# Two sets of fifteen tiny loads on the sync queue of a cached-attention and MLP decode kernel

## The chip, the cores and the metric

The kernel runs on one core of a Trainium2 chip. The metric is the device time of one execution in microseconds (us). The kernel before has a median of 211.23 us over two runs (211.19 to 211.27).

## What is computed

One decode step: a layer norm of the input, then a grouped-query attention over a window of a key/value cache, and beside it a small MLP, summed. Cut to what matters:

```python
# x: 4 x 1 x 576; k_cache, v_cache: 4 x 16 x 8192 x 128; wq: 576 x 4096; wo: 4096 x 576
# w1, w2: 576 x 576; w3: 576 x 4608; w4: 4608 x 576; all bfloat16
def _A_ref(x, k_cache, v_cache, wq, wo):
    W = min(4096, max(256, Sk // 4))                  # 2048 positions
    q = (x @ wq).reshape(B, Sq, Hq, Dh).transpose(0, 2, 1, 3)
    k = jnp.repeat(k_cache[:, :, Sk - W:, :], rep, axis=1)
    v = jnp.repeat(v_cache[:, :, Sk - W:, :], rep, axis=1)
    p = _softmax(jnp.einsum("bhqd,bhkd->bhqk", q, k) * (Dh ** -0.5), axis=-1)
    o = jnp.einsum("bhqk,bhkd->bhqd", p, v)
    return o.transpose(0, 2, 1, 3).reshape(B, Sq, Hq * Dh) @ wo

def _B_ref(x, w1, w2, w3, w4):
    ...
    x1 = x + hs
    h2 = _gelu(_layernorm(x1, axis=-1) @ w3) @ w4
    return x1 + h2

xn = _layernorm(A_x)
return A_x + _A_ref(xn, ...) + _B_ref(xn, ...)
```

With a sequence of one position the padded shifts of the MLP's first part are all zeros, so hs is zero, and w1 and w2 don't enter the result. The kernel before never reads them.

## The kernel before

The 16 key/value heads are worked through one at a time. For each head there is a key tile K and a value tile V, each of 128 partitions with 16 KB, 2 MB in all; the 128 partitions hold four batch entries of 32 row groups, and the tiles live in one pool of six buffers (tag kv). The weights come in larger pieces: wq (4.5 MB), four quarters of wo (wo0 to wo3, 1.1 MB each), w3 (5 MB) and w4 (5 MB in six pieces, with 128 of its rows split off into a small tile called x4). wq, w3 and w4 take turns in one buffer.

All of these loads, except for the input's, are issued by one engine, SP, on the sync queue, in an order written out by hand: the schedule is manual, and an engine runs its instructions in the order of the program. `flush_loads` (L568) walks the list `order`: K0, K1, K2, V0, K3, V1, K4, V2, w3, K5, V3, K6, wo1, V4, and so on, with a quarter of wo ahead of every fourth value tile. Around the two places of the change the order is K9, V7, K10, wo2, V8, K11 ... and, at the end, V13, two x4 rows, V14, three small x4 loads, V15, three x4 rows of one partition, and the six pieces of w4 (`load_w4`, L147, issued by L153). `load_kv` (L100) issues a key or value tile by L103; `x4_rows` (L160) issues the small loads by L164 (20 partitions), L167 (4), L170 (12) and L174 (1).

The loop over t = 0 to 15 (L591) works on several heads at once: it transposes and scores K of head t (DVE L256, PE L369), takes the softmax of head t-1, multiplies head t-2 by its V (PE L426), and scales, sums and projects heads t-3 and t-4. At the end of an iteration `flush_loads` is called again for the buffers that came free, those of K(t) and V(t-2). SP then waits, load by load, for the engine that last read the buffer.

There is a second thing that an issue on SP waits for. Each DMA reports its landing on a semaphore, and the framework that builds the program hands out eight of these semaphores in turn over the DMAs, in program order. An issue that takes a semaphore waits until the DMA that had it before, eight places earlier, has landed, unless SP has already waited for that landing or a later one on it. These waits stand in the built program's list of SP instructions.

The kernel ends with the last heads' remaining steps, the matmuls with w4 as its pieces land (`mlp_out`, PE L215), two copies to the output tile (L684, L686) and its store (L687).

The pool `pad` (L75) holds a tile of 384 bytes per partition that nothing reads or writes.

Of the kernel before, what the change touches and what calls it, by code (L numbers as in the profile page):

```python
# [11 lines left out]
BF16 = mybir.dt.bfloat16  # L12
F32 = mybir.dt.float32
# [5 lines left out]
PAD = 96  # L19
# [3 lines left out]
def kernel(  # L23
# [14 lines left out]
    nc = tc.nc  # L38
    P = 128
# [33 lines left out]


    pad = ctx.enter_context(tc.tile_pool(name="pad", bufs=1))  # L75
    pad.tile([P, PAD], F32, name="pad")
    kvp = ctx.enter_context(tc.tile_pool(name="kv", bufs=NKV))
    wp = ctx.enter_context(tc.tile_pool(name="w", bufs=1))
    wop = ctx.enter_context(tc.tile_pool(name="wo", bufs=2))
# [20 lines left out]
    def load_kv(kind, h):  # L100
        win = k_win if kind == "K" else v_win
        t = kvp.tile([P, NC, Dh], BF16, tag="kv", name=f"{kind.lower()}n")
        nc.sync.dma_start(out=t[:].rearrange("p c d -> p (c d)"),  # L103
                          in_=win[:, h].rearrange("b (p c) d -> p b (c d)", c=NC))
        kv_tiles[kind, h] = t
# [17 lines left out]
    def load_wo(p):  # L123
        t = wop.tile([P, WOR, D], BF16, tag="wo", name="wo_sb")
        nc.sync.dma_start(out=t[:].rearrange("p i n -> p (i n)"), in_=wo_src[p])
        wo_tiles[p] = t

    def load_w3():
        t = wp.tile([P, KJ * F + F // 2], BF16, tag="w", name="w3_sb")
        nc.sync.dma_start(out=t[:, 0:KJ * F], in_=B_w3[0:KJ * P, :].rearrange("(p j) f -> p (j f)", j=KJ))  # L130
        nc.sync.dma_start(out=t[:, KJ * F:], in_=B_w3[KJ * P:D, :].rearrange("r (e f) -> (r e) f", e=2))
        w_tiles["w3"] = t
# [14 lines left out]
    def load_w4():  # L147
        t = wp.tile([P, NFM, D], BF16, tag="w", name="w4_sb")
        for lo, hi in zip(W4_PIECES, W4_PIECES[1:]):
            e = lo // NFH  # L150
            n = NFH - e
            src = B_w4[e * (F // 2):e * (F // 2) + P * n, :].rearrange("(p i) n -> p i n", i=n)
            nc.sync.dma_start(out=t[:, lo:hi, :], in_=src[:, lo - e * NFH:hi - e * NFH, :])  # L153
        w_tiles["w4"] = t

    def load_x4():
        t = kvp.tile([P, NC, Dh], BF16, tag="kv", name="x4")
        w_tiles["x4"] = t[:].rearrange("p c d -> p (c d)")

    def x4_rows(part):  # L160
        t = w_tiles["x4"]
        if part == "A":
            src = B_w4[X0 + 28:F, :].rearrange("(q g i) n -> g q (i n)", q=4, g=5)
            nc.sync.dma_start(out=t[0:NX, XA * D:XS * D], in_=src)  # L164
        elif part == "B":
            src = B_w4[X0:X0 + 16, :].rearrange("(q i) n -> q i n", q=4)[:, 3]
            nc.sync.dma_start(out=t[0:4, (XB + 3) * D:XC * D], in_=src)  # L167
        elif part == "C":
            src = B_w4[X0 + 16:X0 + 28, :].rearrange("(q g) n -> g q n", q=4)
            nc.sync.dma_start(out=t[0:12, XC * D:XA * D], in_=src)  # L170
        else:
            q, lo, hi = part
            src = B_w4[X0 + 4 * q + lo:X0 + 4 * q + hi, :].rearrange("(q i) n -> q (i n)", q=1)
            nc.sync.dma_start(out=t[q:q + 1, (XB + lo) * D:(XB + hi) * D], in_=src)  # L174
# [86 lines left out]
    for kb in range(NQD):  # L261
        nc.gpsimd.tensor_copy(out=sel[:, :, :, kb, :],
                              in_=ident_bf[:].rearrange("p (ib i e) -> p ib e i", ib=2, e=2))
# [19 lines left out]
    with nc.allow_low_precision("zeros and ones"):  # L283
# [7 lines left out]
                          in_=sel_j[:].unsqueeze(1).to_broadcast([P, NG, NJ]))  # L291
# [38 lines left out]
    for r in range(2):  # L330
        nc.vector.tensor_copy(out=q_bf[:, r],
                              in_=qT_ps[:, r].rearrange("p u (g x) -> p g u x", g=NQD)[:, :, :, 0:B])
# [235 lines left out]
    def flush_loads():  # L568
        while pos["n"] < len(order) and pos["free"] > 0:
            kind, h = order[pos["n"]]  # L570
            if kind == "V" and h % WOQ == 0:
                load_wo(h // WOQ)
            if kind == "X":
                load_x4()
            else:
                load_kv(kind, h)
            if kind == "X" or kind == "V" and h > min(X_AFTER):
                for part in X_AFTER.get(h, []):
                    x4_rows(part)
            pos["n"] += 1  # L580
            pos["free"] -= 1
            if (kind, h) == W3_AFTER:
                load_w3()
        if pos["n"] == len(order):
            pos["n"] += 1
            load_w4()

    flush_loads()
    G_AT = 7
    k_transpose(0, 0)  # L590
    for t in range(Hkv):  # L591
# [50 lines left out]
        if hv >= 0:  # L642
            pos["free"] += 1
        flush_loads()

    hl = Hkv - 1
# [71 lines left out]
```

## Time and profile before

| | |
|---|---|
| median of the runs | 211.23 us |
| span of the profiled execution | 209.5 us |
| PE busy | 150.2 us (72%) |
| DVE busy | 113.3 us (54%) |
| ACT busy | 34.9 us (17%) |
| bytes moved by DMA | 87.31 MB, mean 417 GB/s |
| mean granted TensorE clock | 0.868 |
| issue to landing, median: K tiles, V tiles | 25.8 us, 23.0 us |
| SP's longest totals of waiting, L103 | for DVE L387 32.2 us, for PE L426 30.3 us |

The profile is of one execution. The page divides its span into 40 slices and shows, for each engine and for the DMA engines together, the busy share in tenths. A chain of waits is followed back from the last instruction. SPq is SP's own queue: an entry there is the time that an issue took on SP, not the transfer. Time to landing is counted from the issue, so it holds the time that a load stood behind others.

### The profile page before, as it was taken

Reading aid. Unit: us, or ns where it says so; the run is one execution under the profiler, and the core shown is the slowest. Engines: PE = TensorE matmul, PEld = TensorE weight load, DVE = VectorE, ACT = ScalarE, POOL = GpSimd, SP = SyncE. Lnnn points to the kernel's source line nnn. Section 1 sums busy time; section 2 is a strip of 40 time slices with the busy share of each in tenths; the row PEclk is TensorE's granted clock in tenths of the full one; section 3 lists DMA queues with packets and bytes.
Section 4 is the critical chain, followed back from the end, with each engine's and each line's share of the span. In section 5 each row is a group of like instructions: output and inputs, shape, how many; then the busy total and the mean of one; then the engine's idle time right before and its main releaser. Section 6 shows DMA issues by size and latency. Waiting matters only on the chain.

```text
span 209.5 us, 2370 instructions
## 1 busy us (share of the span) xinstructions
PE 150.2 (72%) x972; PEld 57.8 (28%) x972; DVE 113.3 (54%) x156; ACT 34.9 (17%) x72; POOL 9.0 (4%) x32
## 2 busy tenths in 40 slices
PE   0457297698690039759998998589696856999783
PEld 0122132233130003213454332224132312343451
DVE  4511877794910083926607889276849390764110
ACT  7602201112010011110222321102111201023100
POOL 4710000000000000000001200000000000000000
PEclk9999589999797556985999999799879985699699
DMA  7999999999999999999999999999999999999992
GB/s 301 400 422 429 425 429 432 422 438 427 456 422 409 446 419 420 444 444 410 441 422 432 444 405 435 438 444 410 438 429 425 428 445 419 432 438 425 427 407 92
DMA packets 6708, 87.31 MB, mean 417 GB/s; under 512 B 761, under 2 KB 1042, under 8 KB 1706
## 3 DMA queue, kind: packets, MB, share of 16 engines
q1 hardware_dynamic: 6690, 87.17, 97.7%
q8 instruction: 7, 0.11, 0.2%
q10 hardware_dynamic: 8, 0.00, 0.0%
q14 instruction: 3, 0.02, 0.0%
HBM read 87.17 MB, written 0.00 MB: 416 GB/s over the span
## 4 chain that ended last, share of the span: by engine, by line
DMA 76%; PE 18%; DVE 3%; ACT 1%; SPq 1%; issue 1%; DVEq 0%; ACTq 0%
DMA vn<-in_A_v_cache_dram 51%; DMA kn<-in_A_k_cache_dram 12%; DMA w_sb<-in_B_w_dram 7%; DMA wq_sb<-in_A_wq_dram 6%; PE S L369 6%; PE O L426 3%; PE g_ps L499 2%; DVE kt L256 2%; PE q_ps L313 2%; PE oT L439 1%; PE acc L215 1%; PE S L391 1%; DVE qz L345 1%; PE gT_ps L521 1%; SPq L153 1%
## 5 line engine op out<-in xcount | busy, mean ns | idle before, releaser
L369 PE MATMUL S<-kt,qz 128*128 128x512 bf16 x256 | 77.6, 432 | 31.6 <-DVE kt L256 31.6
L256 DVE STREAM_TRANSPOSE kt<-kn 128x2048 int32<-128x2048 int32 x32 | 73.5, 2298 | 25.4 <-DMA kn<-in_A_k_cache_dram 24.0
L369 PEld LDWEIGHTS <-qz 128*128 128x128 bf16 x256 | 23.3, 105 | 64.7 <-issue 47.3
L426 PE MATMUL O<-vn,PT 128*32 128x512 bf16 x256 | 24.3, 424 | 9.7 <-DMA vn<-in_A_v_cache_dram 9.6
L398 ACT ACTIVATE E<-S 128x512 bf16<-128x512 f32 x16 | 9.5, 597 | 73.5 <-PE S L391 73.5
L433 ACT ACTIVATE O_sb<-O,rd 128x512 f32<-128x512 f32 x16 | 11.0, 686 | 63.8 <-DVE rd L416 48.3
L403 DVE STREAM_TRANSPOSE PT<-E 128x512 bf16<-128x512 bf16 x16 | 11.4, 710 | 14.4 <-ACT E L398 14.4
L449 DVE TENSOR_REDUCE on<-oT 128x8 bf16<-128x128 f32 x16 | 4.6, 288 | 22.0 <-PE oT L439 21.9
L426 PEld LDWEIGHTS <-PT 128*32 128x32 bf16 x256 | 5.7, 95 | 33.2 <-issue 22.1
L439 PE MATMUL oT<-ident_w,O_sb 128*128 128x128 f32 x64 | 12.7, 335 | 0.0
L375 DVE TENSOR_REDUCE mx<-S 128x1 f32<-128x512 f32 x16 | 10.5, 657 | 0.9 <-PE S L369 0.9
L439 PEld LDWEIGHTS oT<-ident_w,O_sb 128*128 128x128 f32 x64 | 8.3, 167 | 5.1 <-issue 4.7
L391 PE MATMUL S<-nm,j_row 8*128 8x512 bf16 x16 | 6.8, 428 | 1.8 <-DVE nm L387 1.7
L357 PE MATMUL S<-negbig,ohT 4*128 4x512 bf16 x16 | 6.4, 398 | 0.0
L313 PE MATMUL q_ps<-wq_sb,xnT 128*32 128x512 bf16 x40 | 4.1, 591 | 2.2 <-DMA wq_sb<-in_A_wq_dram 2.2
L215 PE MATMUL acc<-w_sb,gT 128*4 128x288 bf16 x70 | 4.9, 286 | 1.1 <-DMA w_sb<-in_B_w_dram 1.1
L499 PE MATMUL g_ps<-w_sb,ln2T 128*32 128x512 bf16 (+2 forms) x55 | 5.5, 439 | 0.0
L541 POOL TENSOR_TENSOR g_u<-g_x 128x180 f32<-128x180 f32 x1 | 0.5, 486 | 102.5 <-ACT g_x L535 102.5
L215 PE MATMUL acc<-wo_sb,op 128*4 128x288 bf16 x64 | 4.6, 286 | 0.4 <-DVE op L471 0.4
L537 DVE COPY g_x<-gT_ps 128x64 f32<-128x64 f32 x2 | 0.5, 225 | 8.1 <-PE gT_ps L521 8.1
L215 PEld LDWEIGHTS <-gT 128*4 128x4 bf16 (+3 forms) x90 | 3.8, 83 | 3.1 <-issue 1.6
L240 PE MATMUL tp<-ident_bf,first 4*128 4x4 bf16 x8 | 0.6, 172 | 5.3 <-DVE first L227 5.3
(94 smaller groups left out, 79.1 us busy)
## 6 DMA issues: line engine op xcount, KB each, us to landing
kn<-in_A_k_cache_dram SPq DMA_DIRECT2D x16, 2048.0 KB, 25.8
vn<-in_A_v_cache_dram SPq DMA_DIRECT2D x16, 2048.0 KB, 23.0
wo_sb<-in_A_wo_dram SPq DMA_DIRECT2D x4, 1152.0 KB, 38.0
w_sb<-in_B_w_dram SPq DMA_DIRECT2D x1, 4608.0 KB
wq_sb<-in_A_wq_dram SPq DMA_DIRECT2D x1, 4096.0 KB
w_sb<-in_B_w_dram SPq DMA_DIRECT2D x1, 2592.0 KB, 10.9
w_sb<-in_B_w_dram SPq DMA_DIRECT2D x2, 576.0 KB, 34.6
w_sb<-in_B_w_dram SPq DMA_DIRECT2D x1, 864.0 KB
```

What stands on the lines that cost most here:

```text
L215: nc.tensor.matmul(out=acc_of(i), lhsT=lhsT, rhs=rhs[:, i * CW:(i + 1) * CW], start=False, stop=False, skip_group_check=True)
L256: nc.vector.transpose(out=kt[:], in_=src)
L313: nc.tensor.matmul(out=q_ps[r][g * QD:(g + 1) * QD, :], lhsT=xnT[:, k, :], rhs=wq_sb[:, col:col + NW], start=(j == 0), stop=False, skip_gr ...
L369: nc.tensor.matmul(out=S_ps[h][:], lhsT=qz[:, z0:z0 + P], rhs=kt[:, ib, c0:c0 + SC, e:2 * QD:2].rearrange("p c k -> p (c k)"), start=False ...
L375: nc.vector.reduce_max(out=mx[:], in_=S_ps[h][:], axis=AX.X)
L391: nc.tensor.matmul(out=S_ps[h][:], lhsT=j_row[:], rhs=st.pop(("nm", h))[:, 0:1].to_broadcast([NJ, NW]), start=False, stop=False, skip_grou ...
L398: nc.scalar.activation(out=E[h][:].rearrange("p c k -> p (c k)"), in_=S_ps.pop(h)[:], func=ACT.Exp, scale=scale, accum_out=st["rs"][:, h % ...
L403: nc.vector.transpose(out=PT[h][:], in_=E.pop(h)[:])
L426: nc.tensor.matmul(out=O_ps[h][g * QD:(g + 1) * QD], lhsT=PT[h][:, c, :], rhs=vn[:, :, c, :], start=(s == 0), stop=False, skip_group_check ...
L433: nc.scalar.activation(out=O_sb[h][:], in_=O_ps.pop(h)[:], func=ACT.Copy, scale=st.pop(("rd", h)))
L439: nc.tensor.transpose(out=oT[:, s, :], in_=o[:, s, :], identity=ident_w[:, s * NJ:s * NJ + P])
L499: nc.tensor.matmul(out=out, lhsT=ln2T[:, k, :], rhs=rhs, start=(j == 0), stop=False, skip_group_check=True)
```

## The change

After the value tiles of heads 7 and 15 a new function, `load_marks`, issues fifteen loads on the sync queue. The k-th of them (k from 15 down to 1) takes k rows of w1, of 2 + k elements each, into k partitions of a tile that takes the place of the unused pad: 15 x 17, 14 x 16, and so on to 1 x 3 elements of two bytes. Nothing reads that tile. Each load has columns of its own in it; the second set writes the same places again.

```diff
     pad = ctx.enter_context(tc.tile_pool(name="pad", bufs=1))
-    pad.tile([P, PAD], F32, name="pad")
+    mark = pad.tile([P, 2 * PAD], BF16, name="mark")
...
+    def load_marks():
+        at = 0
+        for k in range(15, 0, -1):
+            n = 2 + k
+            nc.sync.dma_start(out=mark[0:k, at:at + n], in_=B_w1[0:k, 0:n])
+            at += n
+
...
                 load_x4()
             else:
                 load_kv(kind, h)
+            if (kind, h) == ("V", 15):
+                load_marks()
             if kind == "X" or kind == "V" and h > min(X_AFTER):
                 for part in X_AFTER.get(h, []):
                     x4_rows(part)
+            if (kind, h) == ("V", 7):
+                load_marks()
             pos["n"] += 1
```

So the first set stands on SP between V7 and K10, and the second between V15 and the last three x4 rows, with w4 behind those. The instructions of the other engines are the same as before.

## The prediction

> **What bounds the kernel now.** I read the page first: the slices, the queue shares, and the chain that ended last.
>
> ```profile
> DMA  7999999999999999999999999999999999999992
> ...
> q1 hardware_dynamic: 6690, 87.17, 97.7%
> ...
> DMA 76%; PE 18%; DVE 3%; ACT 1%; SPq 1%; issue 1%; DVEq 0%; ACTq 0%
> ```
>
> The sync queue's transfers keep the 16 DMA engines busy in every slice but the first and the last. In the middle they move 405 to 456 GB/s, some 430. A 2 MB key or value tile (2.097 MB) therefore takes 2.097/430 = 4.9 us of the stream. PE is busy for 72% of the span, and it is often the engine that waits. So the kernel is one stream of loads with a tail, and the tail is this, from the chain in order of time:
>
> ```profile
> 166.64 22.96 DMA vn<-in_A_v_cache_dram
> ...
> 191.30 14.51 DMA w_sb<-in_B_w_dram
> 205.81 0.04 issue
> 205.85 1.06 PE acc L215 x12
> 206.91 0.43 DVE fin L684
> ```
>
> V14 was issued at 166.64 and landed at 189.60. The last w4 pieces land at about 206, and only some 3.5 us of work follow. A hole in the stream anywhere before that moves the end by its full length, unless something fills it.
>
> What keeps the stream full is SP's lead. This is SP's timeline around the two places of the change (start, length, issue):
>
> ```profile
> 98.67 0.53 SPq L103 DMA_DIRECT2D vn<-in_A_v_cache_dram  x1
> 102.69 0.54 SPq L103 DMA_DIRECT2D kn<-in_A_k_cache_dram  x1
> 105.08 0.33 SPq L125 DMA_DIRECT2D wo_sb<-in_A_wo_dram  x1
> 112.72 0.54 SPq L103 DMA_DIRECT2D vn<-in_A_v_cache_dram  x1
> 117.38 0.54 SPq L103 DMA_DIRECT2D kn<-in_A_k_cache_dram  x1
> ...
> 179.77 0.57 SPq L103 DMA_DIRECT2D vn<-in_A_v_cache_dram  x1
> 184.77 0.82 SPq L174 DMA_DIRECT2D x<-in_B_w_dram  x3
> ```
>
> 98.67 is V7 and 102.69 is K10, which the tile's own rows show landing after
>
> ```profile
> DMA to landing us min/median/max: 22.9/22.9/22.9
> ```
>
> that is, at 125.6. V7 stands one tile ahead of it and lands 4.9 earlier, at 120.7. When V7 lands, K10, wo2, V8 and K11 are already queued: SP leads by 18 us. V15, issued at 179.77, lands after 14.8 us by the same view, at 194.5, and the first w4 piece was queued at 189.62.
>
> **The wait that the change brings.** It is in SP's list of waits (total, times, longest):
>
> ```profile
> SPq L153 <- DMA vn<-in_A_v_cache_dram: 6.8, 2, 4.0
> ...
> SPq L170 <- DMA vn<-in_A_v_cache_dram: 4.6, 1, 4.6
> SPq L174 <- DMA vn<-in_A_v_cache_dram: 4.4, 1, 4.4
> SPq L167 <- DMA wo_sb<-in_A_wo_dram: 2.3, 1, 2.3
> ```
>
> These small loads read and write nothing that a value tile or wo touches. They wait because the eight completion semaphores are handed out in turn and an issue waits until the load eight places earlier has landed. With big loads that rule is harmless, since eight of them are some 35 us of stream. With fifteen tiny ones in a row it is not: in the changed program's list, the eighth tiny load of each set (8 partitions) waits for the value tile just ahead of the set, V7 or V15. SP issues in order, so nothing else can be queued behind that tile until it has wholly landed, and by then every earlier load has landed too. The stream runs dry twice.
>
> **First set, at V7.** The first seven tiny loads (15 to 9 partitions) wait for older loads, the last of them K9, one tile ahead of V7 (about 115.8); they go out before 120.7, under the stream: nothing on the path. Then comes the hole, from V7's landing to K10's data: eight issues (8, 7, 6, 5, 4, 3, 2 and 1 partitions), K10's issue, and the way from issue to data. The issue costs have these nearest rows:
>
> ```profile
> L174 SPq DMA_DIRECT2D x<-in_B_w_dram x5: 240/249/427, 164.0 to 185.3; - x5
> L164 SPq DMA_DIRECT2D x<-in_B_w_dram x1: 907/907/907, 163.0 to 163.0; - x1
> L167 SPq DMA_DIRECT2D x<-in_B_w_dram x1: 248/248/248, 170.0 to 170.0; - x1
> L170 SPq DMA_DIRECT2D x<-in_B_w_dram x1: 837/837/837, 174.9 to 174.9; - x1
> ```
>
> One partition (L174) and four (L167) cost 0.25; twelve (L170) 0.84, twenty (L164) 0.91. Three one-partition issues in 0.82 give 0.29 from start to start, so 0.04 between issues. The bounds for eight are 8 x 0.29 = 2.3 us and 8 x 0.95 = 7.6 us. I take 0.29 for 8, 4, 2 and 1 partitions and 0.88 for 7, 6, 5 and 3, because the cheap rows are counts that are powers of two and the dear ones are not: 4 x 0.29 + 4 x 0.88 = 4.7. It may instead be the dear rows' rearranged sources that cost, and then 2.3 is right.
>
> The restart: the first load of the kernel, 512 KB into an empty queue, landed after 3.3 us, of which 0.524/430 = 1.2 is transfer, so 2.1 us go to the way in and the report of landing. Below, the start's fine windows show the first bytes in 1.50 to 1.75, 0.8 after that issue at 0.74. I take 2.1, since the hole holds both ends: V7's report and K10's way in. K10 waits for the eighth tiny load's slot as well; that lands 2.1 after its issue, under the seven issues that follow (1.8 to 6.7).
>
> The hole is 4.7 + 2.1 = 6.8 us (3.1 to 9.7). Compute doesn't pay again: by 128 the work on K9 and V7 is done, so SP can queue K10, wo2, V8, K11, V9 and K12 at once, 27 us of stream, and the lead is back. Nor does it give back: the stream was full before and is full after.
>
> **Second set, at V15.** The first three wait for V13 and the small x rows, the fourth (12 partitions) for V14, 4.9 us ahead of V15; three more issues follow under V15's own transfer. The eighth waits for V15. After it: the same eight issues, then the three x rows of L174 that now stand behind them (0.82), then w4 and its way in. The hole is 4.7 + 0.8 + 2.1 = 7.6 us (3.9 to 10.5). In the kernel of before SP was stopped here too, but by V14 (L153's 6.8), with V15 still moving. PE's work on V15 falls into this hole and doesn't matter; w4's landing stays last, with the same tail.
>
> **The rest.** The bytes (2 x 1480 elements of two bytes, 6 KB) and their 240 short rows stand in the rings behind V7 and V15 and run in the holes: nothing. The tile mark has the bytes of the tile that it replaces, nobody reads it, and the other engines' instructions are unchanged: nothing.
>
> **The sum.** 6.8 + 7.6 = 14.4 us on the profiled execution's span of 209.5 gives 223.9. The median, 211.23, stands 1.7 above that span, so the time is 225.6 us.
>
> Two rules of the Trainium skill bear on this, both from the page "DMA: Bandwidth & Descriptors". Its section "Issuing engines are not separate DMA queues" says that the time to initiate a DMA on a sequencer is usually small beside the DMA itself; taken as nothing, it would leave 2.1 + 2.1 + 0.8 and 216. The rows speak against it here, since eight issues follow each other with the queue empty. Its section "Anatomy of one DMA" puts a fixed 2.0 us on each DMA; paid one after the other by 30 loads, that would be an estimate of 60 us and 271. Three issues in 0.82 us speak against that.
>
> **The rivals.**
> (a) All tiny issues are cheap, at 0.29: 2.3 + 2.1 and 2.3 + 0.8 + 2.1, 9.6 us, 220.9; with the short restart of 0.8 it is 7.0 and 218.2. For it: four partitions cost no more than one, and the marks' sources are plain rows. Chance 0.28.
> (b) All are dear, at 0.95: 9.7 + 10.5 = 20.2, 231.4. For it: the rows' odd byte counts (34 down to 6), which no row of before has. Chance 0.12.
> (c) One hole only: the tail hides the second, because PE and not w4 is last. PE's waits for w4 pieces are short (1.1 us in all), which speaks for it; but w4's 70 matmuls at a mean of 0.286 us are busy for 4.9 us in all, far less than the 12 us that its pieces (5.16 MB) take to land. 211.2 + 6.8 = 218.0. Chance 0.05.
> (d) Not slower: the slot wait doesn't reach V7's and V15's landings, because the semaphore is satisfied earlier. Then fifteen issues, at most 15 x 0.95 = 14 us, lie under the 22 us from V7's issue to its landing, and SP still leads; set two delays w4's issue by some of 14 us against V15's 14.8. Price 0 to 0.8, time 211 to 212. It decides as soon as K10 goes out before 120.7. Against it: L170 did wait for a value tile. Chance 0.04.
>
> The main case has 0.5, and 0.01 is left for anything else. The range of 219.5 to 230.5 holds the main case with its restart from 0.8 up, most of (a) and part of (b); (c) and (d) fall below. A change of 2% is 4.2 us, about what a measurement of this kernel tells from none: faster 0.01 (nothing above leads there), the same 0.04 (d), slower 0.95.
>
> **What would show it.** In the changed kernel's profile, two DMA slices fall well below 9, near 120 to 127 and 201 to 209; SP's waits gain L160 on vn, about 5 us and more each, with K10 issued after 125 instead of 102.69; the mark's rows give the issue times by size, which settle (a) and (b). Wrong would be K10 issued before V7 lands, DMA slices of 9 throughout, or PE late after the holes, with the stream waiting for buffers.

## The result, and the profile after

The changed kernel takes 224.91 us (median of two runs, 225.55 and 224.26) against 211.23 before: a ratio of 1.0648, 95% interval 1.0575 to 1.0721. The profiled execution has a span of 223.8 us, 14.3 more than before's 209.5. The page's slices, the sync queue's share and the chain by engine:

```profile
DMA  7999999999999999999992799999999999972992
...
q1 hardware_dynamic: 7170, 87.18, 92.3%
...
DMA 71%; DVE 13%; PE 12%; SPq 1%; ACT 1%; issue 1%; DVEq 0%; ACTq 0%
```

The bytes are the same (87.18 MB against 87.17), but the queue's share falls from 97.7% to 92.3%, and slices below 9 stand in two places: near 120 us and near 202 us. The stream ran dry twice. SP's timeline (start, length, issue; a merged row holds the waits between its issues too) shows who let it:

```profile
97.43 0.54 SPq L103 DMA_DIRECT2D vn<-in_A_v_cache_dram  x1
98.01 25.15 SPq L160 DMA_DIRECT2D mark<-in_B_w_dram  x15
123.27 0.54 SPq L103 DMA_DIRECT2D kn<-in_A_k_cache_dram  x1
123.90 0.54 SPq L125 DMA_DIRECT2D wo_sb<-in_A_wo_dram  x1
...
186.78 0.56 SPq L103 DMA_DIRECT2D vn<-in_A_v_cache_dram  x1
191.59 12.33 SPq L160 DMA_DIRECT2D mark<-in_B_w_dram  x15
203.97 1.44 SPq L181 DMA_DIRECT2D x<-in_B_w_dram  x3
205.46 3.16 SPq L153 DMA_DIRECT2D w_sb<-in_B_w_dram  x6
```

K10 goes out at 123.27 instead of 102.69, because SP is among the tiny loads for 25 us. Its waits say on what:

```profile
SPq L160 <- DMA vn<-in_A_v_cache_dram: 22.3, 6, 4.6
...
SPq L160 <- DMA kn<-in_A_k_cache_dram: 9.1, 2, 4.5
...
SPq L181 <- DMA mark<-in_B_w_dram: 0.7, 1, 0.7
```

A tiny load reads w1 and writes a tile of its own, and yet the tiny loads wait 31 us for key and value tiles. The last of those waits in each set ends with V7's or V15's landing. The hole itself, by the microsecond (length, busy time of PE, PEld, DVE, ACT and POOL, granted clock, DMA share, GB/s):

```profile
117.00:118.00 1.00, 1.00 (x5) 0.30 (x4) 0.19 (x2) 0.69 (x2) 0.00 (x0) 1.00 0.99 426
118.00:119.00 1.00, 1.00 (x9) 0.54 (x9) 1.00 (x2) 0.00 (x0) 0.00 (x0) 1.00 0.61 231
119.00:120.00 1.00, 1.00 (x12) 0.22 (x9) 1.00 (x1) 0.00 (x0) 0.00 (x0) 1.00 0.30 115
120.00:121.00 1.00, 0.72 (x10) 0.28 (x3) 1.00 (x2) 0.00 (x0) 0.00 (x0) 1.00 0.02 0
...
123.00:124.00 1.00, 0.94 (x9) 0.56 (x9) 0.99 (x3) 0.00 (x0) 0.00 (x0) 1.00 0.01 0
124.00:125.00 1.00, 0.82 (x3) 0.30 (x4) 0.27 (x1) 0.52 (x2) 0.00 (x0) 1.00 0.98 262
125.00:126.00 1.00, 1.00 (x8) 0.31 (x7) 0.71 (x1) 0.17 (x2) 0.00 (x0) 1.00 0.63 262
126.00:127.00 1.00, 1.00 (x12) 0.21 (x9) 0.00 (x0) 0.00 (x0) 0.00 (x0) 1.00 0.98 410
```

The engines run empty from 118 on, move nothing from 120 to 124, and need until 126 to reach 400 GB/s again. PE and DVE are busy through the hole with heads whose tiles have already landed; the hole is the stream's alone.

The trace's semaphore records give the landing of each load on each of the 16 DMA engines. From them, the first and the last engine of a few loads (us):

```
                 before              changed           last engine later by
V7          118.85  120.80      118.87  120.62          -0.2
K10         123.72  125.64      130.29  131.09           5.4
V9          141.06  142.91      147.69  148.35           5.4
K12         145.91  147.77      152.55  154.75           7.0
V15         192.44  194.52      199.55  201.38           6.9
last of w4  204.56  206.53      219.60  220.15          13.6
```

A tile has landed when the last engine has it, and on the last engine there are three steps, not two: at K10, between V9 and K12, and at w4. On the first engine the second step is missing: K10 is 6.6 later there, and so is K12. The end of the span adds 0.7 more (it comes 3.0 us after the last landing before, 3.65 after).

### The profile page after: what moved, and what is told of

It is laid out like the page before. It is cut to its first block, busy times and chain, and to the rows that moved or that the text cites. A ratio compares the mean times of both kernels' runs of the same rounds, so it can differ in the third digit from the quotient of the medians.

```text
span 223.8 us, 2387 instructions
## 1 busy us (share of the span) xinstructions
PE 150.6 (67%) x958; PEld 58.6 (26%) x972; DVE 113.4 (51%) x156; ACT 34.8 (16%) x72; POOL 9.0 (4%) x32
## 3 DMA queue, kind: packets, MB, share of 16 engines
q1 hardware_dynamic: 7170, 87.18, 92.3%
HBM read 87.17 MB, written 0.00 MB: 390 GB/s over the span
## 4 chain that ended last, share of the span: by engine, by line
DMA 71%; DVE 13%; PE 12%; SPq 1%; ACT 1%; issue 1%; DVEq 0%; ACTq 0%
DMA kn<-in_A_k_cache_dram 53%; DVE kt L263 10%; DMA vn<-in_A_v_cache_dram 7%; DMA wq_sb<-in_A_wq_dram 6%; DMA w_sb<-in_B_w_dram 4%; PE acc L222 3%; PE g_ps L506 2%; PE S L376 2%; PE q_ps L320 2%; DMA mark<-in_B_w_dram 1%; SPq L103 1%; DVE mx L382 1%; DVE qz L352 1%; PE gT_ps L528 1%; DVE PT L410 1%
## 5 line engine op out<-in xcount | busy, mean ns | idle before, releaser
L376 PE MATMUL S<-kt,qz 128*128 128x512 bf16 x242 | 76.6, 438 | 41.0 <-DVE kt L263 38.9
L376 PEld LDWEIGHTS <-qz 128*128 128x128 bf16 x256 | 23.8, 107 | 72.0 <-issue 55.2
L446 PE MATMUL oT<-ident_w,O_sb 128*128 128x128 f32 x64 | 12.2, 325 | 0.0
L382 DVE TENSOR_REDUCE mx<-S 128x1 f32<-128x512 f32 x16 | 10.5, 657 | 0.9 <-PE S L376 0.9
L222 PE MATMUL acc<-w_sb,gT 128*4 128x288 bf16 x70 | 6.7, 374 | 5.8 <-DMA w_sb<-in_B_w_dram 5.8
L695 DVE CAST fin<-acc 4x288 bf16<-4x288 f32 x1 | 0.4, 446 | 14.3 <-PE acc L222 14.3
L222 PEld LDWEIGHTS <-gT 128*4 128x4 bf16 (+3 forms) x90 | 4.5, 101 | 9.9 <-issue 7.0
```

The source lines that it names most:

```text
L222: nc.tensor.matmul(out=acc_of(i), lhsT=lhsT, rhs=rhs[:, i * CW:(i + 1) * CW], start=False, stop=False, skip_group_check=True)
L376: nc.tensor.matmul(out=S_ps[h][:], lhsT=qz[:, z0:z0 + P], rhs=kt[:, ib, c0:c0 + SC, e:2 * QD:2].rearrange("p c k -> p (c k)"), start=False ...
L382: nc.vector.reduce_max(out=mx[:], in_=S_ps[h][:], axis=AX.X)
L446: nc.tensor.transpose(out=oT[:, s, :], in_=o[:, s, :], identity=ident_w[:, s * NJ:s * NJ + P])
```

## The experiments

Each run stands beside runs of the kernel before on the same chip; the ratios are to those, with a 95% interval. The theory on trial: SP waits for the load eight places earlier, so a set that puts the next big load eight places behind a tile makes the stream run dry, and the price is the issues that follow the wait plus a restart. The main rival: a tiny load has a price of its own, 13.7/30 = 0.46 us.

**Six and seven loads after V7.** In both, the set after V15 is gone; the six are the larger loads, the seven the smaller.

```diff
-        for k in range(15, 0, -1):
+        for k in range(15, 9, -1):      # six
+        for k in range(7, 0, -1):       # seven
```

> One set of six tiny loads (15 to 10 partitions) after V7, none after V15. Theory (the stream runs dry because the eighth load after V7 waits for V7's landing): K10 is now the seventh and does not wait for V7, only wo2 does, with K10's 4.9 us still moving; no hole, 211.2 to 211.6 us. Rival (each tiny load has a price of its own, 13.7/30 = 0.46 us): 211.2 + 2.7 = 214.0.

> One set of seven tiny loads (7 to 1 partitions) after V7, one more than the run with six, but fewer rows in all (28 against 75). Theory: K10 is now the eighth load after V7 and waits for its landing; the hole is the restart alone, 2.9 us by the changed kernel's K10, so 214.1; and if a program fetch that comes after the drain holds up one engine again, as in the changed kernel, 1.4 more, 215.5. Rival (0.46 a load): 214.4, and 0.5 above the run with six; a rival that goes by rows would have it below that run.

Six: 211.73 against 211.17 us, ratio 1.0033 (1.0019 to 1.0047), 0.1 above the theory's end. Seven: 215.49, ratio 1.0206 (1.018 to 1.0232). One more load, with fewer rows in all, costs 3.8 us; the six together cost 0.6. SP's timelines, with six:

```profile
98.70 0.53 SPq L103 DMA_DIRECT2D vn<-in_A_v_cache_dram  x1
99.28 11.96 SPq L160 DMA_DIRECT2D mark<-in_B_w_dram  x6
115.86 0.54 SPq L103 DMA_DIRECT2D kn<-in_A_k_cache_dram  x1
120.70 0.36 SPq L125 DMA_DIRECT2D wo_sb<-in_A_wo_dram  x1
```

and with seven:

```profile
98.42 0.53 SPq L103 DMA_DIRECT2D vn<-in_A_v_cache_dram  x1
99.01 16.99 SPq L160 DMA_DIRECT2D mark<-in_B_w_dram  x7
120.65 0.54 SPq L103 DMA_DIRECT2D kn<-in_A_k_cache_dram  x1
121.29 0.55 SPq L125 DMA_DIRECT2D wo_sb<-in_A_wo_dram  x1
```

With six, K10 waits for K9's landing and is queued at 115.86, 4.8 us ahead of V7's landing; it is wo2 that then waits for V7, with K10 on its way. With seven, K10 itself waits for V7 and goes out at 120.65. SP's waits for value tiles after the tiny loads say the same, wo2's issue (L125) with six and K10's (L103) with seven:

```profile
SPq L125 <- DMA vn<-in_A_v_cache_dram: 4.2, 1, 4.2
SPq L103 <- DMA vn<-in_A_v_cache_dram: 4.6, 1, 4.6
```

In the seven's trace V7 landed at 120.59 and K10 at 128.18: 7.59, against 4.84 before. The restart alone, which holds K10's own issue of 0.54, is thus 2.75 us. It is not the whole of the 4.3; the rest is in the next experiment but one.

**Each set alone.**

```diff
-            if (kind, h) == ("V", 15):
-                load_marks()
```

(first set alone; for the second set alone, the other two lines go instead)

> The fifteen loads after V7 alone. Theory: 8 issues behind the wait at 0.33 and a restart of 2.9 make 5.6 us, with the fetch's 1.4 it is 7.0: 216.8 to 218.3, K10 issued 2.6 us after V7's landing. Rival (0.46 a load): 218.1. The engines' landings of one tile, which lie within 0.8 us after the drain, should come apart to about 2 us at the next fetch of program code.

> The fifteen loads after V15 alone. Theory: 8 issues (2.6), three x rows (0.8, or 1.5 if a program fetch stands before a tiny load that one of them waits for), restart 2.7, and a tail 0.7 longer where PE comes back from idling: 6.8 to 7.5, 218.0 to 218.7. Together with the run that has the first set alone it should make up the changed kernel's 13.7 within 1 us. Rival (0.46 a load): 218.1; rival (the tail hides the second set): 211.5.

The first alone: 218.00, ratio 1.032 (1.0302 to 1.0337), 6.8 us. The second alone: 218.40, ratio 1.0338 (1.0315 to 1.0361), 7.2 us. Together 14.0 against the change's 13.7: the two holes add up, and the tail doesn't hide the second. In the second set alone too one x row waited 1.0 us for a tiny load (SP's waits: L181 for mark), after a read of program code that began at 195.62. By themselves these two runs don't speak against the price per load, which also gives 218.1.

**The third step: seven loads 30 us earlier, after V4.** The trace has a queue of its own for program code, seven reads of 16 KB, some 0.95 us each. In the changed kernel one starts at 152.28, just at the third step:

```profile
q1 hardware_dynamic: 46, 0.51, 94.2%
q8 instruction: 1, 0.02, 4.5%
```

(DMA view of 152 to 153.3: queue, packets, MB, share). If the step belongs to the first such read after the hole, it moves with the hole.

```diff
-        for k in range(15, 0, -1):
+        for k in range(7, 0, -1):
...
-            if (kind, h) == ("V", 15):
-                load_marks()
...
-            if (kind, h) == ("V", 7):
+            if (kind, h) == ("V", 4):
```

> Seven loads (7 to 1 partitions) after V4 and no others, as in the run with seven after V7 but 30 us earlier. Theory: the restart, 2.75 us, and then 1.2 to 1.6 for the first program fetch after the drain: 4.0 to 4.4, 215.2 to 215.6. The landings of a tile on the 16 engines should lie within 0.8 us after V4 (at about 92) and come apart to about 2 us at the fetch near 105, with no further step at the fetch near 150. Rival (the step belongs to the place near 150, or to K12): apart at 150 again. Rival (no such thing, restart alone): 214.0.

215.11 against 211.25, ratio 1.0179 (1.0161 to 1.0197), 0.1 below the range. The restart, worked out as before, is 2.5 here: K7 landed 7.39 us after V4, against 4.88. The landings of a tile on the 16 engines, in us after the first of them, from the semaphore records, first as the changed kernel has them and then this run:

```
changed, V9    0.00 0.04 0.05 0.06 0.09 0.10 0.11 0.22 0.26 0.27 0.30 0.37 0.38 0.44 0.51 0.67
changed, K12   0.00 0.04 0.05 0.06 0.09 0.10 0.10 0.22 0.26 0.29 0.30 0.35 0.36 0.47 0.64 2.20   (read of code at 152.28)
after V4, V5   0.00 0.02 0.03 0.04 0.05 0.06 0.07 0.08 0.13 0.21 0.24 0.25 0.31 0.33 0.45 0.58
after V4, K8   0.00 0.02 0.03 0.05 0.06 0.07 0.08 0.08 0.13 0.26 0.31 0.32 0.32 0.38 0.54 1.79   (read of code at 107.32)
```

Exactly one engine of sixteen falls 1.2 to 1.6 us back, at the first 16 KB read of code after the hole, and the step moved from 150 to 107 with the hole; at the read near 150 this run's spread stays at 1.7 to 1.8. The first set alone, the seven after V7 and the run below show the same (0.62 to 2.20, 0.69 to 1.91, 0.43 to 1.89). By the last engine the whole stream is that much later. The kernel before pays this once, at a read near 30 us (0.54 to 1.80); at the later ones other engines fall back to where the first one is already, and the spread stays near 1.9. A hole makes all engines start level again, and the next read of code counts anew. The other fifteen show nothing at the read: on the first engine the seven loads after V7 have cost 4.0 us at K10 already (127.70 against 123.72) and 4.0 at K12. That the read sits on the very engine that falls back is inferred: the records don't name the engine.

**What made an issue dear.** Fifteen loads after V7 alone, all of 12 rows in L170's way.

```diff
-            nc.sync.dma_start(out=mark[0:k, at:at + n], in_=B_w1[0:k, 0:n])
+            src = B_w1[0:12, 0:n].rearrange("(q g) n -> g q n", q=4)     # n = 12
+            nc.sync.dma_start(out=mark[0:12, at:at + n], in_=src)
```

> Fifteen loads after V7 alone, each of 12 partitions with 12 elements, from a source rearranged in the way of L170's (rows taken in another order than they lie). If the rearranged source made L170 and L164 dear, each takes 0.82 to 0.9 us on SP and the eight behind the wait 6.9 to 7.5: with a restart of 2.9 and the fetch's 1.4, 11.2 to 11.8, 222.4 to 223.0. If the dear rows were dear for their longer rows, each takes 0.3 and the time is that of the first set alone, 218.0.

221.72, ratio 1.0484 (1.046 to 1.0508): 10.5 us, 0.7 below the expected range. Its mark rows and SP after V7's landing:

```profile
L161 SPq DMA_DIRECT2D mark<-in_B_w_dram x15: 704/705/872, 99.5 to 126.0; - x15
```

```profile
120.73 5.95 SPq L161 DMA_DIRECT2D mark<-in_B_w_dram  x8
126.78 0.58 SPq L103 DMA_DIRECT2D kn<-in_A_k_cache_dram  x1
```

An issue of 12 rows takes 0.71 us with the rows in another order, and 0.30 in the changed kernel with the rows as they lie. So the rearranged source is what was dear, not a count that is no power of two; it differs from the plain one in the order of its rows and in having one more dimension, and no run tells these two apart. The remaining 0.1 to L170's 0.84 was not taken further. And the price follows the issues behind the wait: 6.0 us for eight, where the plain ones took 2.65.

**The same thirty loads, kept from piling up.** First on SP, two after each of the fifteen tiles from V7 to V15; then both sets issued by GpSimd, whose loads take other semaphores.

```diff
+            if ("V", 7) in order[:pos["n"] + 1] and kind != "X":
+                load_marks()        # two loads a call
```

> All thirty loads, same shapes and same queue, but two after each of the fifteen tiles from V7 to V15. Theory (the stream runs dry because the eighth load after a tile waits for that tile): eight places back is now at least two tiles of stream ahead, nothing runs dry, 211.2 to 212.5 us, with SP's lead cut to 10 us. Rival (0.46 us for each tiny load): 224.9 as in the changed kernel.

```diff
-            nc.sync.dma_start(out=mark[0:k, at:at + n], in_=B_w1[0:k, 0:n])
+            nc.gpsimd.dma_start(out=mark[0:k, at:at + n], in_=B_w1[0:k, 0:n])
```

> The same two sets of fifteen, issued by GpSimd, which takes other semaphores, instead of SP. Theory: SP's order and its waits are those of before, 211.2 to 211.8 us, the short rows cost nothing. Rival (the short rows themselves hold up the stream): 218 or more.

Spread: 213.95 against 211.25, ratio 1.0117 (1.0092 to 1.0142). The price per load is out, since 13.7 have become 2.7, but the run lies 1.5 above what the theory allowed. In its trace the tiles up to V14 land within 0.2 us of before's times, and V15 1.7 later. SP's timeline shows V15's issue late, at 186.53 instead of 179.77:

```profile
184.81 0.82 SPq L181 DMA_DIRECT2D x<-in_B_w_dram  x1
185.68 0.75 SPq L165 DMA_DIRECT2D mark<-in_B_w_dram  x2
186.53 0.58 SPq L103 DMA_DIRECT2D vn<-in_A_v_cache_dram  x1
```

SP waited for V13's landing at 184.80, and V15 went out only 1.5 us before the first engine was done with V14 (187.98). The stream didn't run dry, but some rows moved around that moment took 0.7 to 1.6 us in the records instead of 0.61. That V15's late issue is what made them slow is argued from the times, not shown by a run. Nor is it shown that this is all of the 2.7: the profiled run was the shortest of four (213.17).

By GpSimd: 212.16, ratio 1.0039 (1.0024 to 1.0054), 0.4 above the expected end. GpSimd has no tile to wait for and issues its sets earlier than SP would, at 11 to 24 us and at 117 to 129. So this run bounds the price of the short rows under a full stream, at 0.9 us for both sets and the whole of GpSimd's part in it; it says nothing of their place.

**The same step at V15.** There is no set after V7, and three or four loads after V15.

```diff
-        for k in range(15, 0, -1):
+        for k in range(3, 0, -1):       # or range(4, 0, -1)
```

> Three tiny loads (3 to 1 partitions) after V15, none after V7. Theory: the first piece of w4 is the seventh load after V15 and waits for the 12-partition load ahead of it, not for V15; only the second piece waits for V15, with the first piece's 6 us moving: no hole, 211.2 to 212.0. Rival (0.46 us a load): 212.6.

> Four tiny loads (4 to 1 partitions) after V15, one more than the run with three. Theory: the first piece of w4 is now the eighth load and waits for V15; the hole is the restart, 2.7 us, with no tiny issue in it, and 1.2 to 1.6 more if the program fetch near 199 comes after the restart, and up to 0.7 in the tail: 213.9 to 216.2. Rival (0.46 us a load): 213.1, and 0.5 above the run with three.

Three: 212.16 against 211.39, ratio 1.0042 (1.0025 to 1.0059), 0.2 above the expectation's end. Four: 214.99, ratio 1.0177 (1.0161 to 1.0193). One load more costs 2.8 us. With three, w4's first piece is queued under V15's transfer:

```profile
180.04 0.56 SPq L103 DMA_DIRECT2D vn<-in_A_v_cache_dram  x1
...
191.01 5.94 SPq L153 DMA_DIRECT2D w_sb<-in_B_w_dram  x6
```

With four, at V15's landing, 194.49, with no tiny issue left behind the wait:

```profile
179.80 0.57 SPq L103 DMA_DIRECT2D vn<-in_A_v_cache_dram  x1
...
194.50 3.33 SPq L153 DMA_DIRECT2D w_sb<-in_B_w_dram  x6
```

The last of w4 lands 15.63 us after V15, against 12.01 before. These 3.6 are more than a restart of 2.5 to 3.0; a read of code at 197.68 falls into this one, and what it adds was not measured by itself.

## Why the prediction was right, and where it was not

The mechanism was right at each point that decides: the eighth place behind V7 and V15 (the steps from six to seven and from three to four), two holes that add up (each set alone), the tail that hides nothing, the lead that is back at once, and short rows that cost at most 0.9 us for both sets under a full stream. The sum of 14.4 us met the profiled 14.3, and the forecast of 225.6 the median of 224.9. That it came so close is luck: the terms inside were off, and they made up for each other (us):

| term | predicted | measured in the profiled run |
|---|---|---|
| eight issues, at V7 and at V15 | 4.7 and 4.7 | 2.65 and 2.6 |
| restart, at V7 and at V15 | 2.1 and 2.1 | 3.0 and 2.7 |
| three x rows before w4 | 0.8 | 1.5 |
| engines out of step again | none | 1.5 |
| tail after the last landing | none | 0.7 |
| drift of the landings of V7 and V15 | none | -0.3 |
| sum | 14.4 | 14.3 |

**The issues.** The step that was wrong is "the cheap rows are counts that are powers of two and the dear ones are not". The changed kernel's rows decide it:

```profile
L160 SPq DMA_DIRECT2D mark<-in_B_w_dram x30: 250/293/638, 98.0 to 203.7; - x30
```

Every plain issue behind the wait is cheap, with 7 rows as with 8, and eight take 2.65 from start to start, so that K10 went out at 123.27 and not after 125, as the prediction's sign had it. (The 638 is the first load, of 15 rows; in the second set it took 0.35.) The twelve rearranged rows show what was dear. So rival (a), with its 2.3, was right on this term, and the prediction had named the reason ("the dear rows' rearranged sources") and put it second. That the total of (a) was nevertheless too low is the doing of the restart, the x rows, the step and the tail, the rows of the table that follow. The range held not most of (a), as the prediction says, but about half: (a) went from 218.2 to 220.9, and the range began at 219.5.

**The restart** was mis-sized: 2.75 and 2.5 where it stands alone (seven loads, after V7 and after V4), and 3.0 and 2.7 here. The first load of the kernel, from which the 2.1 came, was a load of 512 KB; at a hole's end the windows above show two microseconds at 262 GB/s. How much of the difference comes from that was not measured. The Trainium skill's page "DMA: Bandwidth & Descriptors", section "Anatomy of one DMA", has about 2.0 us of fixed cost for a load of GpSimd's path, not for each DMA, as the prediction put it. These loads are SP's, and their restarts measure 2.5 to 3.0.

**The x rows** took 1.5 and not 0.8, since one of them waited 0.7 for the slot of a tiny load. That one landed late, at 204.88, after a read of code that began at 202.57; that the read held it up is inferred from the times. The prediction also misread the wait of before: of L153's 6.8 us only the longest, 4.0, was for V14. The other 2.8 was for V15, by the fifth piece of w4, the eighth load behind V15.

**Out of step.** "Nor does it give back: the stream was full before and is full after" missed that a hole takes something more: the level start of the engines makes the next read of code count. Between V9 and K12 that is the 1.5 of the table; with the seven loads after V7 it is 1.2, most of what lies between the 2.75 and the 4.3.

**The tail.** PE idles from 208.4 to 214.25 while it waits for w4, and when it comes back its granted clock is 0.50 and then 0.77 (the figure before the DMA share), where before it was 1.00 throughout the matmuls with w4:

```profile
214.00:216.00 2.00, 1.75 (x16) 0.98 (x17) 0.00 (x0) 0.00 (x0) 0.00 (x0) 0.50 0.99 416
216.00:218.00 2.00, 2.00 (x20) 1.06 (x18) 0.00 (x0) 0.00 (x0) 0.00 (x0) 0.50 1.01 420
218.00:220.00 2.00, 2.00 (x30) 1.26 (x26) 0.00 (x0) 0.00 (x0) 0.00 (x0) 0.77 0.74 279
```

The w4 matmuls have a mean of 374 ns against 286, and PE ends 0.9 us after the last landing instead of 0.4. These 0.5 of the 0.7 are read off the trace; no run was made on them.

Of the rivals, (b) fell with the issues' rows, (c) with the second set alone, and (d) with K10's issue at 123.27. What the page "DMA: Bandwidth & Descriptors" says in its section "Issuing engines are not separate DMA queues", that the time to initiate a DMA is usually small beside the DMA itself, holds for the first seven issues of each set, which go out under the stream, and not for the eight behind the wait, which took 2.65 us of an empty stream.

Open: the 0.6 and 0.8 us of the runs with six and three loads, and the part of the 2.7 in the spread run beyond V15's late issue. With six, the ten runs lie between 211.50 and 212.53, and in the profiled one (212.53) an engine that was already last falls 0.8 further back before V14, but no run was made to tell what sets that.

## What to carry to other kernels

When a kernel is one stream of loads, count the places in the issuing engine's list: if completion semaphores go round, each tiny load takes a place that a 2 MB load would have used, and the lead in bytes shrinks to what stands in the last eight places. Keep the next big load fewer than eight places behind a big one, and look for the step in the program's own list of waits, since the profile of before shows it only as a small load that waits for a tile it has nothing to do with. And price a hole in the stream by its restart, 2.5 to 3.0 us here, before counting the issues in it.

## What the runs showed of the hardware that was not expected

By the last engine, a hole costs more than its length: it levels the 16 engines, and at the next 16 KB read of program code one of them falls 1.2 to 1.6 us behind again, and the whole stream with it (five of five runs with a hole at V4 or V7). Without a hole the kernel pays for that once, at the first of its seven reads (0.54 to 1.80), and at the others the spread stays near 1.9.

A load from a rearranged source costs SP 0.71 us to issue for 12 rows, where the same count of plain rows costs 0.30.
